# Four chunks of a fused attention and FFN kernel as two pairs: seven block products for eight, with weight sums streamed from HBM

## The chip, the cores and the metric

The kernel runs on one core of a Trainium2 chip. The core's engines run side by side, each with its own queue taken in order: TensorE (PE; PEld is its weight load), VectorE (DVE), ScalarE (ACT), GpSimd (POOL) and SyncE (SP), whose queue issues the DMAs. The metric is the device time of one execution in microseconds (us).

## The reference

```python
def attention(q, k, v, mem_k, mem_v):           # B 4, H 8, S 768, D 64
    for c in range(S // 32):                     # each 32 queries see 16 keys left, 8 right, 8 memory keys
        k_full = concat(mem_k, k[c*32-16 : c*32+32+8]); v_full = ...
        a = softmax(0.125 * q[c*32:c*32+32] @ k_full.T)
        out[c*32:c*32+32] = a @ v_full
x = out as (3072 tokens, 512)
h = x @ w_in                                     # 512 -> 2048, the first FFN matrix
g = s * relu(h)**2 + b
y = g @ w_out                                    # 2048 -> 512, the second
```

All in float32; a product is made of three TensorE matmuls on rounded high and low parts (low x high, high x low, high x high).

## The kernel before

The 3,072 tokens are 8 chunks of 384. A chunk needs 4 visits of attention (two heads each) and 16 steps of the FFN, one per slice f of 128 hidden units. A visit (`attend`, `weights`, `flip`) puts scores on TensorE (L383), maxima on VectorE (L440), exponentials on ScalarE (L444), a normalisation on GpSimd (L450), transposes on VectorE (L470) and values on TensorE (L415). From chunk 2 on, the values of one visit and the scores of the next are issued as one group.

A step is 12 matmuls of the hidden product (`hidden`, L510: 4 row blocks of the weight slice x 3 parts, 384 columns each), then relu, square, affine and the high part gH on ScalarE (L517 to L520), the low part gL on VectorE (L521), and 9 matmuls of the result (`result`, L532: 3 token tiles x 3 parts, 512 columns), one step later on TensorE. After the last step of a chunk the three accumulators are copied (L548) and stored.

The weights come as 64-bit floats. `weight` loads one 0.5 MB tile (L485) into one of 16 early tiles or a ring of four named words, joins the bits on ScalarE and VectorE (L487 to L492, through a ring wv) and leaves a high and a low part w (L496, L497). All 32 weight tiles then stay on chip.

`Plan` sets the order: every operation has a priority (in steps) and dependencies, and a list scheduler with a table of durations lays each engine's queue out before the program runs. On the chip each queue is then taken in that order. The planner keeps some VectorE and GpSimd operations (marked lock) apart.

Of the kernel before, what the change touches and what calls it, by code (L numbers as in the profile page):

```python
# [25 lines left out]
P = 128  # L26
# [38 lines left out]
SLOW, NSLOW = 290.0, 6
# [8 lines left out]
class Val:  # L74
# [170 lines left out]
@with_exitstack  # L245
def body(ctx: ExitStack, tc: tile.TileContext, qkv, w1, w2, out):
    nc = tc.nc
    plan = Plan()
    op = plan.op

# [10 lines left out]
    wts = {}  # L261
    early_tiles = [const.tile([P, 2 * DM], F32, name=f"early{i}", tag=f"slot{i}") for i in range(NEARLY)]

    def weight_tile(half, f):
        if (half, f) not in wts:
            i = LATE_W.index((half, f)) if (half, f) in LATE_W else -1
            wts[half, f] = const.tile([P, 2, DM], F32R, name=f"w{half}_{f}", tag=f"slot{i}" if i >= 0 else f"w{half}_{f}")
# [6 lines left out]
    xr = [[const.tile([P, TOK], F32R, name=f"x{a}{c}_{i}") for a in "HL" for c in range(NC_T)] for i in range(2)]  # L274
    x_ring = Ring(xr)
    wvs = ring("wv", 3, [P, DM], F32)
# [68 lines left out]
    def anchor(ch, c):  # L345

        if ch == 0:
            return -30 + 2 * c
        if ch < NALONE:
            return starts[ch] - LEAD - 2.0 * (H // 2 - 1 - c)  # L350
        return starts[ch] - JOIN - (4.0 if ch > NALONE else APART) * (H // 2 - c)

    x_vals, open_ = {}, []

    def attend(ch, c):
# [11 lines left out]
        due = a if alone else anchor(ch, c + 1)  # L367
# [18 lines left out]
        if alone:  # L386
            for j in range(GB):
                op("PE", "scores", a, lambda j=j: product(j), (raw[0],), (scs[0][j], scs[1][j]))
        else:

            last = open_.pop() if open_ else None
# [13 lines left out]
            (turn if early else flip)(a + n * 0.5, t[n], aT[n], ch == 1 or n == 1)  # L405

        va = Val(ps, "v")
        if c == 0:
            x_vals[ch] = Val(x_ring)
        x = x_vals[ch]  # L410
        av = lambda: va.tile[:, :TOK]

        def value(j):
# [2 lines left out]
                                 v.tile[:, (n * GB + j) * D:(n * GB + j + 1) * D], aT[n].tile[:, j, :], start=True, stop=True)  # L416

        def store():
            op("ACT", "xhigh", due + 0.9, lambda: nc.scalar.activation(x.tile[c], av(), AF.Copy), (va[0],), (x["H", c],))
            op("DVE", "xlow", due + 0.9, lambda: nc.vector.tensor_tensor(x.tile[NC_T + c], av(), x.tile[c].bitcast(F32), ALU.subtract),  # L420
               (va[0], x["H", c]), (x["L", c],))

        def values():
# [76 lines left out]

    g_vals, h_vals, a_vals, partial = {}, {}, {}, {}

    def hidden(u):
        ch, f = STEPS[u]
        h = Val(ps, "h")
        x, w = x_vals[ch], c_w[0, f]

        def products(c):
            for n, (wi, xi) in enumerate(((0, NC_T + c), (1, c), (0, c))):
                nc.tensor.matmul(h.tile[:, :TOK], weight_tile(0, f)[:, wi, c * P:(c + 1) * P], x.tile[xi], start=(c == 0 and n == 0),  # L510
                                 stop=(c == NC_T - 1 and n == 2))
# [5 lines left out]
        op("ACT", "relu", u, lambda: nc.scalar.activation(hp(), hp(), AF.Relu), (), (h[0],))  # L517
        op("ACT", "square", u, lambda: nc.scalar.activation(hp(), hp(), AF.Square), (), (h[0],))  # L518
        op("ACT", "affine", u, lambda: nc.scalar.activation(hp(), hp(), AF.Identity, scale=s_sb, bias=b_sb), (c_s[0], c_b[0]), (h[0],))  # L519
        op("ACT", "high", u, lambda: nc.scalar.activation(g.tile[0], hp(), AF.Copy), (h[0],), (g["H"],))  # L520
        op("DVE", "low", u, lambda: nc.vector.tensor_tensor(g.tile[1], hp(), g.tile[0].bitcast(F32), ALU.subtract),  # L521
           (h[0], g["H"]), (g["L"],))

    def result(u):
# [89 lines left out]
```

## Time and profile before

| | |
|---|---|
| median of 3 runs | 641.81 us (641.69 to 641.99) |
| span of the profiled execution, first to last instruction | 639.8 us |
| median of the runs less that span | 2.0 us |
| busy TensorE / VectorE / ScalarE / GpSimd | 625.7 / 354.8 / 422.4 / 86.9 us |
| DMA | 46.83 MB, mean 73 GB/s |

The busy times are sums over the profiled execution. Matmuls overlap, and their ends are modelled, so a busy TensorE can still have slack; what one matmul really costs is read from the distance of starts.

### The profile page before, as it was taken

Reading aid. Unit: us, or ns where it says so; the run is one execution under the profiler, and the core shown is the slowest. Engines: PE = TensorE matmul, PEld = TensorE weight load, DVE = VectorE, ACT = ScalarE, POOL = GpSimd, SP = SyncE. Lnnn points to the kernel's source line nnn. Section 1 sums busy time; section 2 is a strip of 40 time slices with the busy share of each in tenths; the row PEclk is TensorE's granted clock in tenths of the full one; section 3 lists DMA queues with packets and bytes.
Section 4 is the critical chain, followed back from the end, with each engine's and each line's share of the span. In section 5 each row is a group of like instructions: output and inputs, shape, how many; then the busy total and the mean of one; then the engine's idle time right before and its main releaser. Section 6 shows DMA issues by size and latency. Waiting matters only on the chain.

```text
span 639.8 us, 10842 instructions
## 1 busy us (share of the span) xinstructions
PE 625.7 (98%) x3822; PEld 544.2 (85%) x3826; DVE 354.8 (55%) x1283; ACT 422.4 (66%) x1137; POOL 86.9 (14%) x140
## 2 busy tenths in 40 slices
PE   9998988999999999999999999999999999999997
PEld 5686877888888898888888988889888888989995
DVE  5999999726667355563447554473555725421112
ACT  6999898756766566666566666664666665645543
POOL 4522100101211011110011111110111100100000
PEclk9999999999999999999999999999999999999999
DMA  8933664012112011121103011120111200010001
GB/s 336 404 112 114 212 207 152 2 46 83 58 46 96 5 41 47 47 95 47 45 2 105 37 46 46 46 96 1 45 47 47 96 17 1 1 50 1 1 0 50
DMA packets 17334, 46.83 MB, mean 73 GB/s; under 512 B 1920, under 2 KB 1920, under 8 KB 17280
## 3 DMA queue, kind: packets, MB, share of 16 engines
q1 hardware_dynamic: 17280, 46.15, 20.8%
q8 instruction: 30, 0.49, 0.3%
q14 instruction: 24, 0.20, 0.1%
HBM read 39.85 MB, written 6.29 MB: 72 GB/s over the span
## 4 chain that ended last, share of the span: by engine, by line
PE 80%; DVE 10%; ACT 6%; DMA 4%; issue 1%; SPq 0%; POOL 0%; DVEq 0%
PE ps L532 37%; PE ps L510 36%; PE ps L383 4%; PE ps L415 3%; DVE wv L490 2%; DVE w L497 2%; DVE wv L492 2%; DMA early<-w 2%; ACT t L444 1%; DMA v<-qkv 1%; DVE gL L521 1%; DVE words L488 1%; ACT wv L487 1%; DMA early<-qkv 1%; ACT ps L519 1%; ACT w L496 1%
## 5 line engine op out<-in xcount | busy, mean ns | idle before, releaser
L510 PE MATMUL ps<-xH,w 128*128 128x384 f32 x1024 | 261.8, 337 | 1.3 <-DVE w L497 1.3
L532 PE MATMUL ps<-w,gH 128*128 128x512 f32 x768 | 240.0, 393 | 0.6 <-DVE w L497 0.5
L510 PEld LDWEIGHTS ps<-xH,w 128*128 128x128 f32 x1024 | 186.0, 188 | 7.6 <-DVE w L497 2.4
L521 DVE TENSOR_TENSOR gL<-ps,gH 128x384 fp32r<-128x384 f32 x128 | 70.6, 552 | 208.8 <-ACT gH L520 207.6
L517 ACT ACTIVATE ps<-ps 128x384 f32<-128x384 f32 x128 | 60.9, 475 | 173.1 <-PE ps L510 173.1
L510 PE MATMUL ps<-xL,w 128*128 128x384 f32 x512 | 174.4, 341 | 0.0
L532 PEld LDWEIGHTS ps<-w,gH 128*128 128x128 f32 x768 | 144.0, 188 | 29.4 <-DVE w L497 1.3
L532 PE MATMUL ps<-w,gL 128*128 128x512 f32 x384 | 154.9, 403 | 6.6 <-DVE gL L521 6.6
L470 DVE STREAM_TRANSPOSE aT<-t 32x128 f32<-32x128 f32 x384 | 116.2, 303 | 51.1 <-POOL t L450 46.4
L444 ACT ACTIVATE t<-t,nmax 96x128 f32<-96x128 f32 x256 | 99.3, 390 | 17.2 <-DVE nmax L440 16.9
L510 PEld LDWEIGHTS ps<-xL,w 128*128 128x128 f32 x512 | 96.1, 188 | 6.6 <-ACT w L496 0.4
L532 PEld LDWEIGHTS ps<-w,gL 128*128 128x128 f32 x384 | 72.0, 188 | 24.5 <-DVE gL L521 9.6
L519 ACT ACTIVATE ps<-ps,b_sb,s_sb 128x384 f32<-128x384 f32 x128 | 82.6, 645 | 4.2
L450 POOL TENSOR_TENSOR t<-t,rden 96x512 f32<-96x512 f32 x64 | 68.5, 1070 | 85.8 <-DVE rden L449 85.8
L447 POOL TENSOR_SCALAR rden<-den 96x4 f32<-96x4 f32 x64 | 16.0, 251 | 375.5 <-ACT t L444 372.8
L520 ACT ACTIVATE gH<-ps 128x384 fp32r<-128x384 f32 x128 | 62.9, 491 | 3.9
L518 ACT ACTIVATE ps<-ps 128x384 f32<-128x384 f32 x128 | 60.8, 475 | 4.0
L440 DVE CUSTOM_DVE_ANT_0 t<-ps,mask 96x128 f32<-96x128 f32 x256 | 56.8, 281 | 4.2 <-PE ps L383 3.8
L444 ACT ACTIVATION_READ_ACCUMULATOR t<-t,nmax 96x1 f32 x256 | 48.1, 188 | 0.0
L383 PE MATMUL ps<-raw 64*96 64x128 f32 x448 | 31.8, 279 | 0.0
L383 PEld LDWEIGHTS ps<-raw 64*96 64x96 f32 x448 | 25.3, 159 | 4.1 <-issue 0.8
L415 PEld LDWEIGHTS ps<-aT,v 128*64 128x64 f32 x448 | 19.6, 136 | 7.9 <-issue 6.6
(45 smaller groups left out, 289.3 us busy)
## 6 DMA issues: line engine op xcount, KB each, us to landing
raw<-qkv SPq DMA_DIRECT2D x28, 448.0 KB, 3.3
words<-w SPq DMA_DIRECT2D x22, 512.0 KB, 3.9
v<-qkv SPq DMA_DIRECT2D x28, 256.0 KB, 3.6
out<-partial SPq DMA_DIRECT2D x21, 256.0 KB, 2.1
early<-w SPq DMA_DIRECT2D x10, 512.0 KB, 9.9
early<-qkv SPq DMA_DIRECT2D x3, 448.0 KB, 5.8
early<-qkv SPq DMA_DIRECT2D x4, 256.0 KB, 6.4
out<-wv SPq DMA_DIRECT2D x3, 256.0 KB, 3.8
```

The lines of the kernel that those rows point to most:

```text
L383: nc.tensor.matmul(scv(n)[:, j, :], raw.tile[rows, j * QB:(j + 1) * QB], raw.tile[rows, TOK + j * P:TOK + (j + 1) * P], start=True, stop=True)
L440: op("DVE", "max", a + 0.1, lambda j=j: nc.vector.tensor_tensor_reduce(t.tile[:, j, :], scv()[:, j, :], mask[:, kind(j)], -SCALE, 3.0e38, ...
L444: op("ACT", "exp", a + 0.2, lambda j=j: nc.scalar.activation(t.tile[:, j, :], t.tile[:, j, :], AF.Exp, bias=nmax()[:, j:j + 1], scale=-1.0 ...
L450: op("POOL", "norm", a + 0.25, lambda: nc.gpsimd.tensor_tensor(t.tile, t.tile, rden().unsqueeze(2).to_broadcast([QB, GB, P]), ALU.mult), [ ...
L470: nc.vector.transpose(aT.tile[gg, :, cs], t.tile[cs, :, gg])
L510: nc.tensor.matmul(h.tile[:, :TOK], weight_tile(0, f)[:, wi, c * P:(c + 1) * P], x.tile[xi], start=(c == 0 and n == 0), stop=(c == NC_T - ...
L517: op("ACT", "relu", u, lambda: nc.scalar.activation(hp(), hp(), AF.Relu), (), (h[0],))
L518: op("ACT", "square", u, lambda: nc.scalar.activation(hp(), hp(), AF.Square), (), (h[0],))
L519: op("ACT", "affine", u, lambda: nc.scalar.activation(hp(), hp(), AF.Identity, scale=s_sb, bias=b_sb), (c_s[0], c_b[0]), (h[0],))
L520: op("ACT", "high", u, lambda: nc.scalar.activation(g.tile[0], hp(), AF.Copy), (h[0],), (g["H"],))
L521: op("DVE", "low", u, lambda: nc.vector.tensor_tensor(g.tile[1], hp(), g.tile[0].bitcast(F32), ALU.subtract), (h[0], g["H"]), (g["L"],))
L532: nc.tensor.matmul(acc.tile, g.tile[gi][:, t * P:(t + 1) * P], weight_tile(1, f)[:, wi, :], start=(first and n == 0), stop=(last and n == 2))
```

## The change

Chunks 0 to 3 stay as they were. Chunks 4 and 5, and 6 and 7, become pairs. For a pair the first FFN matrix is computed two slices (f = 2g, 2g + 1) and two chunks at a time: the weights are a 2 x 2 block matrix A, the inputs a 2 x 2 block matrix B (rows: halves of the 512 inputs, columns: the two chunks), and the product is formed from seven block products in place of eight (`seven`). A block product is 6 matmuls of 384 columns.

- `blocks`: for each of 8 groups GpSimd rebuilds the full weights (2 additions of 512 columns, vsum), forms four sums S1 to S4 (4 of 256, ssum), ScalarE and VectorE cut them into high and low parts (1,024 columns each), and 11 DMAs store the group's seven blocks to HBM tiles w1s. 16 further DMAs store the second FFN matrix to w2s. The second matrix and the plain blocks A11, A12, A22 can be stored as soon as a weight tile is ready; the sums wait for all weights.
- `mix`: before a pair, four subtractions of 768 columns on GpSimd and seven cuts on ScalarE and VectorE make T1 to T4 and the parts of B11, B21 and B22, in the places of weight tiles that are no longer needed.
- `word`: weights come back from HBM, 28 tiles of 0.5 MB for the products and 32 for the results of each pair, into 8 slots in the places of old weight tiles.
- `seven`: per group 7 products, five additions on VectorE, a copy and relu on ScalarE, squares of 768 columns on GpSimd and a wide affine on ScalarE. P2 is added onto P1's bank and P4 onto P7's.
- `rest`: the result matmuls of the pair, 2 x 16 units of 9 matmuls, after all products, with gH and gL cut from the stored g.
- The order of the rest: visits of chunks 2 to 5 get anchors 2.3 steps apart from step 18 on, those of chunks 6 and 7 lie in the first pair; two visits are open in place of one (DEPTH); epilogues have a priority 8 steps earlier from step 22 on (AHEAD); wv has 5 buffers in place of 3.

```diff
+STEPS = (... [(ch, f) for ch in range(2, NPLAIN) for f in range(NF)])      # NPLAIN = 4, was NCHUNK
+BLOCKS = ("A11", "S2", "S1", "S3", "A12", "S4", "A22")
...
-        return starts[ch] - JOIN - (4.0 if ch > NALONE else APART) * (H // 2 - c)
+        i = (ch - NALONE) * (H // 2) + c
+        last = (NCHUNK - 2 - NALONE) * (H // 2)
+        if ch < NCHUNK - 2:
+            return VISITS[0] + VISITS[1] * i
+        return base(NCHUNK - 4) + LAST_VISITS[0] + LAST_VISITS[1] * (i - last)
...
+    def blocks(g):
+        full, sums, high, low = (Val(words) for _ in range(4))
...
+            op("POOL", "vsum", due, lambda k=k, f=f: nc.gpsimd.tensor_tensor(
+                at(full, 2 * k, 2), weight_tile(0, f)[:, 0].bitcast(F32), weight_tile(0, f)[:, 1].bitcast(F32), ALU.add),
+               [*parts[k], *all_w], (full[k],), lock=True)
...
+        op("ACT", "shigh", due, lambda: nc.scalar.activation(high.tile.bitcast(F32R), sums.tile, AF.Copy), every, (high[0],))
+        op("DVE", "slow", due, lambda: nc.vector.tensor_tensor(low.tile.bitcast(F32R), sums.tile, high.tile, ALU.subtract),
+           (*every, high[0]), (low[0],), lock=True)
...
+            put = lambda src, dst, reads, key: op("SP", "issue", due + 0.5, lambda: nc.sync.dma_start(dst, src()), reads,
+                                                  (c_w1s[unit][q, key],), size=P * 2 * P * 4)
...
+    def word(ch, n, prio):
+        v = Val(streams)
+        src, c_src = (w1s[n], c_w1s[n]) if n < NWORDS else (w2s[(n - NWORDS) % NF], c_w2s[(n - NWORDS) % NF])
...
+        op("SP", "issue", prio - 3.0, lambda: nc.sync.dma_start(v.tile.bitcast(F32), flat), list(c_src.parts.values()), [v[0], *gone], size=P * DM * 8)
...
+    def seven(ch, g):
...
+            more = name in ("P2", "P4")
+            bank = banks_[name] = banks_[{"P2": "P1", "P4": "P7"}[name]] if more else Val(ps, "p")
+            def matmuls():
+                for kc in range(2):
+                    for i, (wi, xi) in enumerate(((0, 1), (1, 0), (0, 0))):
+                        lo = q * DM + wi * 2 * P + kc * P
+                        nc.tensor.matmul(bank.tile[:, :TOK], w.tile[:, lo:lo + P], xv.tile[xi][:, kc], ...)
...
+        b1 = product("P1", "A11", "B11", 0)
+        op("ACT", "keep", due - AHEAD, lambda: nc.scalar.activation(sb(sa), pt(b1), AF.Copy), (b1[0],), (sa[0],))
+        b6 = product("P6", "S2", "T2", 1)
+        op("DVE", "add", due - AHEAD, lambda: nc.vector.tensor_tensor(sb(su), pt(b6), sb(sa), ALU.add), (b6[0], sa[0]), (su[0],))
+        b5 = product("P5", "S1", "T1", 2)
...
+            op("POOL", "square2", due + 2, lambda v=v: nc.gpsimd.tensor_tensor(v.tile, v.tile, v.tile, ALU.mult), (), (v[0], v[1]), lock=True)
...
+    def rest(ch, i):
+        w, src = word(ch, NWORDS + i, due), gv[c, f // 2]
...
+        op("ACT", "high", due - AHEAD, lambda: nc.scalar.activation(g.tile[0], part(), AF.Copy), (src[f % 2],), (g["H"],))
+        op("DVE", "low", due - AHEAD, lambda: nc.vector.tensor_tensor(g.tile[1], part(), g.tile[0].bitcast(F32), ALU.subtract),
+           (src[f % 2], g["H"]), (g["L"],), lock=True)
...
+    for f in range(NF):
+        op("SP", "issue", LATER + 1.5 * f, lambda f=f: nc.sync.dma_start(w2s[f], weight_tile(1, f).bitcast(F32)),
+           (c_w[1, f]["H"], c_w[1, f]["L"]), (c_w2s[f][0],), size=P * DM * 8)
...
+    for ch in range(NPLAIN, NCHUNK, 2):
+        visits(ch)
+        visits(ch + 1)
+        mix(ch)
+        for g in range(NF // 2):
+            seven(ch, g)
+        for i in range(2 * NF):
+            rest(ch, i)
```

Three places of the engines' queues show what moves. SyncE's queue while the weights are prepared, before: loads of weight tiles stand one behind the other.

```order
L485 DMA words_102<-w 128x1024
L485 DMA words_103<-w 128x1024
L485 DMA words_100<-w 128x1024
L485 DMA words_101<-w 128x1024
L369 DMA raw_105<-qkv 128x896
```

The same place now (w1s and w2s are the HBM tiles, w_5_828 and the like finished weight tiles):

```order
L633 DMA w1s_67<-w_5_828 128x2x256
L533 DMA words_140<-w 128x1024
L418 DMA v_150<-qkv 128x512
L830 DMA w2s_89<-w_4_865 128x1024
L533 DMA words_141<-w 128x1024
L533 DMA words_142<-w 128x1024
L633 DMA w1s_67<-w_6_902 128x2x256
L633 DMA w1s_69<-w_6_902 128x2x256
L830 DMA w2s_90<-w_5_909 128x1024
L533 DMA words_143<-w 128x1024
L633 DMA w1s_70<-w_7_963 128x2x256
```

Stores of finished tiles stand between the loads; between the fifth and the last words load there are 12 of w1s (0.26 MB) and 9 of w2s (0.52 MB).

VectorE's queue just after the last weight tile, before: maxima, transposes and gL alone.

```order
L449 RECIPROCAL rden_121<-rden_121 96x4
L521 TENSOR_TENSOR gL_133<-ps_143,gH_132 128x384
L470 STREAM_TRANSPOSE aT_113<-t_107 32x4x32 x8
L521 TENSOR_TENSOR gL_129<-ps_142,gH_128 128x384
L521 TENSOR_TENSOR gL_131<-ps_139,gH_130 128x384
```

There now (words are reused for the sums: 143 the sums, 140 their high part, 141 their low part):

```order
L497 RECIPROCAL rden_161<-rden_161 96x4
L572 TENSOR_TENSOR gL_173<-ps_183,gH_172 128x384
L518 STREAM_TRANSPOSE aT_153<-t_147 32x4x32 x8
L629 TENSOR_TENSOR words_141<-words_143,words_140 128x1024
L572 TENSOR_TENSOR gL_169<-ps_182,gH_168 128x384
L572 TENSOR_TENSOR gL_171<-ps_179,gH_170 128x384
L629 TENSOR_TENSOR words_141<-words_143,words_140 128x1024
```

The cuts of the weight sums (1,024 columns) stand between the gL, and the next visit's maxima follow two gL sooner.

TensorE's queue at the start of the second pair (before there was no such place: each chunk's hidden and result matmuls alternate). Names again_n are tiles in the places of old weights: again_0 is B11, again_1 B21, again_4 T2, and again_9 to again_11 are stream slots.

```order
L790 MATMUL ps_181<-again_9_3598,gL_173 128x512
L790 MATMUL ps_181<-again_9_3598,gH_172 128x512 x2
L740 MATMUL ps_183<-again_0_3188,again_10_3603 128x384
L740 MATMUL ps_183<-again_0_3187,again_10_3603 128x384 x2
L740 MATMUL ps_183<-again_1_3250,again_11_3642 128x384
L740 MATMUL ps_183<-again_1_3249,again_11_3642 128x384 x2
L740 MATMUL ps_182<-again_4_3607,again_10_3603 128x384
L740 MATMUL ps_182<-again_4_3606,again_10_3603 128x384 x2
```

Behind the last result matmuls of the first pair come P1, then P2 on the same bank, then P6; the last value group of chunk 7 stands 27 result matmuls ahead of P1. (Each product's rows appear twice in the queue, once for each half of the rows; one half is shown.)

## Rows read from the trace of the kernel before

**Rows 1.** The page: busy time by engine, and TensorE's granted clock in 40 slices.

```profile
PE 625.7 (98%) x3822; PEld 544.2 (85%) x3826; DVE 354.8 (55%) x1283; ACT 422.4 (66%) x1137; POOL 86.9 (14%) x140
...
PEclk9999999999999999999999999999999999999999
```

**Rows 2.** Chain of waits, 372 to 400 us: start, duration, what.

```profile
371.85 1.05 PE ps L383 x16
...
375.17 2.10 PE ps L510 x12
...
381.44 2.10 PE ps L532 x9
...
389.82 0.81 PE ps L415 x16
```

**Rows 3.** Windows: length, busy PE, PEld, DVE, ACT, POOL, clock, DMA share, GB/s.

```profile
9.00:27.00 18.00, 17.68 (x188) 12.08 (x189) 15.19 (x95) 17.64 (x77) 11.60 (x18) 1.00 1.03 408
57.00:105.00 48.00, 43.25 (x242) 35.92 (x243) 45.72 (x91) 43.58 (x94) 3.18 (x4) 1.00 0.61 207
113.00:205.00 92.00, 91.20 (x564) 80.42 (x565) 55.17 (x222) 61.29 (x177) 14.05 (x23) 1.00 0.17 58
205.00:560.00 355.00, 355.00 (x2175) 315.96 (x2174) 184.96 (x734) 222.75 (x612) 46.29 (x73) 1.00 0.13 43
```

**Rows 4.** Groups of instructions by line: count, busy us, mean ns, idle before.

```profile
L510 PE MATMUL ps<-xH,w 128*128 128x384 f32 x1024 | 261.8, 337 | 1.3 <-DVE w L497 1.3
...
L510 PE MATMUL ps<-xL,w 128*128 128x384 f32 x512 | 174.4, 341 | 0.0
...
L497 DVE TENSOR_TENSOR w<-wv,w 128x512 fp32r<-128x512 f32 x32 | 22.2, 693 | 1.7 <-ACT w L496 1.7
```

**Rows 5.** Timeline, 601 to 634 us: start, duration, engine, line, operation.

```profile
601.45 0.39 PE L532 MATMUL ps<-w,gL 128*128 128x512 f32 x1
...
601.65 0.47 ACT L517 ACTIVATE ps<-ps 128x384 f32<-128x384 f32 x1 [1.98 <-PE ps L510]
...
603.87 0.56 DVE L521 TENSOR_TENSOR gL<-ps,gH 128x384 fp32r<-128x384 f32 x1 [3.60 <-ACT gH L520]
...
605.64 0.40 PE L532 MATMUL ps<-w,gL 128*128 128x512 f32 x1
...
633.78 0.50 PE L532 MATMUL ps<-w,gL 128*128 128x512 f32 x1 [0.76 <-DVE gL L521]
```

**Rows 6.** Waits of TensorE, 113 to 200 us: total us, times, longest.

```profile
PE ps L532 <- DVE gL L521: 1.7, 2, 0.9
```

**Rows 7.** Timeline, 36 to 39 us: GpSimd's normalisation and VectorE's cut of a weight.

```profile
36.73 1.04 POOL L450 TENSOR_TENSOR t<-t,rden 96x512 f32<-96x512 f32 x1 [1.15 <-DVE rden L449]
...
37.35 0.97 DVE L497 TENSOR_TENSOR w<-wv,w 128x512 fp32r<-128x512 f32 x1
```

**Rows 8.** Timeline, 84 to 92 us: a weight load's issue and its first use.

```profile
84.34 1.67 SPq L485 DMA_DIRECT2D words<-w  x2
...
89.52 0.67 ACT L487 ACTIVATE wv<-words 128x512 f32<-128x512 f32 x1
```

**Rows 9.** DMA: issues in 73 to 105 us (landing us); queue in 560 to 640 us.

```profile
words<-w SPq DMA_DIRECT2D x13, 512.0 KB, 3.2
...
q1 hardware_dynamic: 864, 1.57, 5.3%
```

**Rows 10.** Timeline of a visit, 372 to 388 us, VectorE and ScalarE.

```profile
373.77 0.28 DVE L440 CUSTOM_DVE_ANT_0 t<-ps,mask 96x128 f32<-96x128 f32 x1
...
373.98 0.28 DVE L440 CUSTOM_DVE_ANT_0 t<-ps,mask 96x128 f32<-96x128 f32 x1
...
381.43 2.51 DVE L470 STREAM_TRANSPOSE aT<-t 32x128 f32<-32x128 f32 x8 [0.71 <-POOL t L450]
...
374.55 0.39 ACT L444 ACTIVATE t<-t,nmax 96x128 f32<-96x128 f32 x1
```

**Rows 11.** Waits of TensorE, 56 to 113 us.

```profile
PE ps L532 <- DVE gL L521: 5.1, 7, 0.9
```

More of the change, by code (lines that the diff above doesn't have):

```diff
@@ L389, in attend @@
         else:
[L391 removed]
+            last = open_.pop(0) if len(open_) >= DEPTH else None
             def both():
@@ new lines, in again, with again_x, later, old @@
+    def again(half, f, shape, dtype):
+        return lambda: const.tile(shape, dtype, name=f"again{half}_{f}", tag=weight_tag(half, f))
+    def again_x(old, c):
+        return lambda: const.tile([P, 2, TOK], F32, name=f"againx{old}_{c}", tag=f"x{c}_{x_vals[old].slot}")
+    def later(slots, shape, dtype):
+        return Ring(Lazy([again(*s, shape, dtype) if s[0] in (0, 1) else again_x(*s) for s in slots])), slots
+    def old(slot):
+        if slot[0] in (0, 1):
+            return list(c_w[slot].parts.values())
+        return [x_vals[slot[0]][a, slot[1]] for a in "HL"]
@@ new lines, in body, with first, mix, subtract @@
+    n_of = {}
+    def first(kind, slots):
+        n = n_of[kind] = n_of.get(kind, -1) + 1
+        return old(slots[n]) if n < len(slots) else []
+    XNAMES = ("B11", "B21", "B22", "T1", "T2", "T3", "T4")
+    xc = {}
+    def mix(ch):
+        due = base(ch) - 6.0
+        raw = {name: x_vals[ch + int(name[2]) - 1, int(name[1]) - 1] for name in ("B11", "B12", "B21", "B22")}
+        flat = lambda v: v.tile[:, :2 * TOK] if v.ring is words else v.tile.rearrange("p c t -> p (c t)")
+        both = lambda v: [v[0], v[1]] if v.ring is words else [v[0]]
+        def subtract(dst, a, b, writes, prio):
+            op("POOL", "tsum", due + prio, lambda: nc.gpsimd.tensor_tensor(flat(dst), flat(a), flat(b), ALU.subtract), [*both(a), *both(b)],
+               writes, lock=True)
+        def cut(name, v, prio):
+            n = XNAMES.index(name)
+            x = xc[name] = Val(xcs[n])
+            gone = [p for s in seven_slots[n] for p in old(s)] if ch == NPLAIN else []
+            whole = lambda k: x.tile[k].rearrange("p c t -> p (c t)")
+            op("ACT", "thigh", due + prio, lambda: nc.scalar.activation(whole(0), flat(v), AF.Copy), both(v), [x["H"], *gone])
+            op("DVE", "tlow", due + prio, lambda: nc.vector.tensor_tensor(whole(1), flat(v), whole(0).bitcast(F32), ALU.subtract),
+               [*both(v), x["H"]], [x["L"], *gone], lock=True)
+        def temp():
+            v = Val(temps)
+            return v, [v[0], *first("temp", temp_slots)]
+        cut("B11", raw["B11"], 0.0)
+        cut("B21", raw["B21"], 0.0)
+        cut("B22", raw["B22"], 0.0)
+        t1, w = temp()
+        subtract(t1, raw["B12"], raw["B11"], w, 0.1)
+        cut("T1", t1, 0.2)
+        subtract(raw["B12"], raw["B22"], raw["B12"], both(raw["B12"]), 0.2)
+        cut("T3", raw["B12"], 0.3)
+        t2, w = temp()
+        subtract(t2, raw["B22"], t1, w, 0.4)
+        cut("T2", t2, 0.5)
+        t4, w = temp()
+        subtract(t4, raw["B21"], t2, w, 0.6)
+        cut("T4", t4, 0.7)
@@ new lines, in rest, with products @@
+    def rest(ch, i):
+        c, f = ch + i // NF, i % NF
+        due = base(ch) + NF // 2 * GROUP + UNIT * i
+        w, src = word(ch, NWORDS + i, due), gv[c, f // 2]
+        g = Val(gs)
+        part = lambda: src.tile[:, f % 2]
+        op("ACT", "high", due - AHEAD, lambda: nc.scalar.activation(g.tile[0], part(), AF.Copy), (src[f % 2],), (g["H"],))
+        op("DVE", "low", due - AHEAD, lambda: nc.vector.tensor_tensor(g.tile[1], part(), g.tile[0].bitcast(F32), ALU.subtract),
+           (src[f % 2], g["H"]), (g["L"],), lock=True)
+        def products(acc, t):
+            for n, (gi, wi) in enumerate(((1, 0), (0, 1), (0, 0))):
+                nc.tensor.matmul(acc.tile, g.tile[gi][:, t * P:(t + 1) * P], w.tile[:, wi * DM:(wi + 1) * DM],
+                                 start=(f == 0 and n == 0), stop=(f == NF - 1 and n == 2))
+        for t in range(NT):
+            if f == 0:
+                a_vals[t] = Val(ps, "acc")
+            acc = a_vals[t]
+            op("PE", "result", due, lambda acc=acc, t=t: products(acc, t), (g["H"], g["L"], w[0]), (acc[0],))
+            if f < NF - 1:
+                continue
+            o = Val(outs)
+            op("DVE", "out", due, lambda acc=acc, o=o: nc.vector.tensor_copy(o.tile, acc.tile), (acc[0],), (o[0],))
+            row = c * TOK + t * P
+            op("SP", "issue", due, lambda o=o, row=row: nc.sync.dma_start(out[row:row + P, :], o.tile), (o[0],), (), size=P * DM * 4)
```

171 lines of the change are left out of this document (143 added, 28 removed).

## The prediction

> **What bounds the kernel now.** I read the page first: TensorE is busy for 98% of the span at a granted clock of 1.0 (2.4 GHz) in every slice [rows 1]. Busy TensorE time is no proof, so next the chain of waits over 28 us in the middle: nothing but TensorE, 12 hidden matmuls in 2.10 us, 9 result matmuls in 2.10 us, a visit in 0.81 + 1.05 us, end to end [rows 2]. So a matmul of 384 columns costs 0.175 us, one of 512 columns 0.233 us, and one step (one 128-wide slice of the FFN for one chunk) 4.2 us. The windows show where that holds: from 205 to 560 us TensorE never idles; from 113 to 205 us it idles 0.8 us; in 57 to 105 us it does, and there VectorE is busy for 45.7 of 48 us [rows 3]. That is the weight preparation (four VectorE operations per 0.5 MB weight tile, the last of them 0.69 us [rows 4]), and the DMA engines move only 207 GB/s in it, against 408 GB/s in a saturated stretch [rows 3]. The groups give the count: 1,024 + 512 hidden matmuls [rows 4], 192 per chunk.
>
> The span is 639.8 us and the median of the runs 641.8, so 2.0 us lie around the span; I make the sum on 641.8.
>
> **The change, part by part.**
>
> *Removed from TensorE.* Four chunks had 4 x 192 = 768 hidden matmuls. Two pairs now have 8 groups x 7 products x 6 matmuls = 336 each, 672 together, all of 384 columns with one weight load each as before. 96 x 0.175 = **-16.8 us**. The 9 result matmuls per slice and the visits stay. From 205 us on nothing else bounds the kernel [rows 3], so this comes off the end if TensorE stays fed.
>
> *The end.* Before, the last step waits 0.76 us for its own gL: squaring, scaling and cutting follow the last hidden product [rows 5]. In the new result stage these inputs were made three units ahead. **-0.8 us**. The copies and stores behind it stay.
>
> *Epilogues ahead of exponentials from step 22.* From 113 to 200 us TensorE waited twice for gL, at most 0.9 us each [rows 6]; the windows give 0.8 us of idle [rows 3]. **-0.4 us** (0 to -0.8).
>
> *Start of the second pair.* The order puts the last value group of chunk 7 only 27 result matmuls (3 x 2.10 = 6.3 us) ahead of P1, then P2, then P6. P2 adds onto P1's bank, so it waits until ScalarE has copied P1 away: an activation of 384 columns is 0.47 us, and a hop between engines about 0.2 us each way (TensorE goes on to the next product at 601.45 us, ScalarE starts on the last at 601.65 us [rows 5]): **+0.9 us**. P6 needs T2 = B22 - T1. From the last value: hop and copy 0.7, then on GpSimd B22 - B12 and T2, each 768 elements. The nearest row is its normalisation, 1.04 us for 512 [rows 7], so 1.6 us each (3.2 with a hop), then cut on ScalarE and VectorE, some 0.9 + 1.1 us by proportion, and three hops: about 6.7 us. P6 starts at 6.3 + 1.05 + 0.9 + 1.05 = 9.3 us. It fits with 2.6 us to spare, but the two cuts before it and the three copies of results stand ahead on VectorE; bounds 0 to +3.
>
> *Weight preparation, 57 to 105 us.* SyncE's queue now holds between its 18 weight loads 12 stores of 0.26 MB and 9 of 0.52 MB, 7.9 MB, that wait in order for finished weight tiles. The old traffic is 207 GB/s x 48 us = 9.9 MB. At 407 GB/s all 17.8 MB need 43.7 us of the 48: it fits, at 91%. A load issued at 84.34 us was first used at 89.52 us, and the median landing there is 3.2 us [rows 8, 9]: 2.0 us of slack; a store of 0.52 MB ahead of it costs 1.3 us. Three of the 18 loads have 1.05 MB of stores directly ahead (2.6 us), so 3 x 0.6 = 1.8 us is the price in the queue. **+1.0 us** (0 to +8, see the rival). That stores run near the rate of loads is borne out by the only ones there are: 1.57 MB took 5.3% of 16 engines' 80 us, 370 GB/s while busy [rows 9], against 408 / 1.03 = 396 GB/s for loads [rows 3]. No store with 1 KB pieces exists before.
>
> The Trainium skill (DMA: Bandwidth & Descriptors, Specifications) gives a limit of about 358 GB/s of HBM for one core; the 408 GB/s held for 18 us [rows 3] contradict it, and the measurement decides. By the page 17.8 MB would take an estimated 49.7 us, 1.7 us more than the window, and my sum would be 0.7 us higher.
>
> *Steps 20 to 54: denser visits and weight sums.* Visits for chunks 2 to 5 now come every 2.1 steps, that is every 2.1 x 4.2 + 1.9 = 10.8 us. VectorE per visit: 8 maxima at 0.21 pace, 16 transposes in 2 x 2.51, and a cut like gL's 0.56: 7.3 us [rows 5, 10]; plus 2.1 gL, 1.2, plus for one block the cut of 1,024 elements, 1.4 us from 0.69 for 512 [rows 4]: 9.9 of 10.8 us. ScalarE: 8 exponentials of 0.39 and a copy, 3.6 [rows 10]; plus 2.1 epilogues of some 2.1 us (from 601.65 us to gL's start at 603.87 us [rows 5]), plus 1.2 for the high parts: 9.2 us. GpSimd, 2.5 before, gets about 4.2 more. All fit, VectorE barely (60% in 113 to 205 us before [rows 3]). TensorE is in order, so it stalls where a transpose or a gL is late. A visit's transposes end 11 us after its scores [rows 2, 10]; with two visits open instead of one they may take 21 us, so ten are free. A gL has 1.2 us to spare (ready at 604.43 us, wanted at 605.64 us [rows 5]). Eight blocks put a 1.4 us operation in front of some gL, and it may itself wait for GpSimd: once a VectorE cut took 0.97 us instead of 0.69 while GpSimd's normalisation was running [rows 7]. Bound: 8 x 1.4 = 11 us, if each blocks a gL wholly; nothing if each falls in a gap. A visit's eight transposes are 0.315 us each, so a gL gets in between them in time; only the 1.4 us cuts are longer than the slack, and only by 0.2 us when they run alone. I take a value near the lower end: **+1.5 us** (0 to +11).
>
> The Trainium skill (SBUF — State Buffer, Who interferes with whom) says that a VectorE instruction with two SBUF inputs and a GpSimd instruction that reads SBUF exclude one another for their whole length. The 0.97 us of [rows 7] agree. This speaks against the change, which adds 86 such VectorE instructions (8 weight cuts, 14 x cuts, 64 result cuts) and some 90 GpSimd ones; by that rule alone, each of the 8 weight cuts waiting out a GpSimd addition of an estimated 1.04 us, some 8 us would come on top of my sum, and C below would be the forecast.
>
> *Hidden.* The streams: 60 tiles of 0.5 MB per pair, one per 2.1 us of TensorE, 250 GB/s of the 408 shown, with 8 slots, so issued 15 us before use; eight in flight at the full rate are 8 x 0.52 / 0.408 = 10 us. Without that cover each tile late costs its lateness. Per group of products (7.4 us of TensorE) GpSimd squares 2 x 1.6 us, ScalarE works some 4.5 us by proportion from 0.47 us for 384 columns [rows 5], VectorE adds 5 x 0.56 us; what they make is used at the earliest one group later. The mix for pair 1: chunk 5's last value stands six steps (25 us) ahead of P1.
>
> Sum: 641.8 - 16.8 - 0.8 - 0.4 + 0.9 + 1.0 + 1.5 = 627.2, say **627 us**.
>
> **The rivals.**
> *A, the forecast*: 621.5 to 629. Its lower end: no added stall and 2 us less of the 5.1 us for which TensorE waits for gL in 56 to 113 us [rows 11], since five wv buffers instead of three let ScalarE run ahead. Chance 0.62.
> *B, the weight window becomes bound by DMA*: if stores of 1 KB pieces move at 250 GB/s while loads keep 407, the window needs 24.4 + 31.4 = 55.8 us, +8; at 300, +2.6. For it: 91% load, one in-order queue. Against: the 370 GB/s. 629 to 635 us. Chance 0.12.
> *C, vector side too dense*: the 11 us of steps 20 to 54 in full, 637 us. For it: 9.9 of 10.8 us, and only 1.2 us of slack for a gL. Chance 0.15.
> *D, slower*: the mechanism of B further on. The window must grow by 17 us to eat the gain: 24.4 + 7.9 / r = 65 gives r = 194 GB/s. Below that the kernel is slower; at 150 GB/s 77 us, so about 655 us. Nothing in the rows is so slow. Chance 0.07.
> *E, the streams starve*: at 200 GB/s a tile takes 2.6 us against 2.1, 120 x 0.5 = 60 us. The rate that the rows show is twice that. Chance 0.02.
>
> **How the numbers follow.** A measurement of this kernel tells about 0.2% (1.3 us) from no change. A, B and C are faster by more: 0.89. D and E are slower: 0.09. The rest, 0.02, is a C or D that stops at the old time. The likeliest is A: 627 us. The range takes A, B and C with its bound: 621.5 to 637, some 0.85 of the chance.
>
> **What would show it.** Hidden matmuls 768 of 384 columns plus 672 in the products at the same 0.175 us; TensorE without idle slices past 120 us; the weight preparation ending near 116 us as before (later: B or D); 250 GB/s from about 290 us on; in steps 20 to 54 few waits of TensorE for gL or transposes (many of about 1 us: C); about 1 us at the second pair's start; the last result matmuls without a wait. I am wrong if loads of weights land later than 5 us in 57 to 105 us, if gL waits pass 5 us in total, or if result units wait for a stream.

## The result and the profile after

The changed kernel takes 632.06 us (median of 4 runs, 631.11 to 632.25), the kernel before 641.75 us beside it: ratio 0.9844, interval 0.9831 to 0.9858. That is 9.7 us faster; 14.6 were forecast. The profiled execution has a span of 629.3 us, 10.5 less than before, so it is compared with -14.6 too.

The page of the changed kernel (busy time by engine; then issues: count, KB, us to landing) answers to [rows 1]:

```profile
PE 611.6 (97%) x3730; PEld 526.0 (84%) x3730; DVE 424.2 (67%) x1369; ACT 406.1 (65%) x1063; POOL 200.1 (32%) x228
...
PEclk9999999999999999999999999999999999999999
...
L560 PE MATMUL ps<-x,w 128*128 128x384 f32 x768 | 148.5, 340 | 1.3 <-DVE w L545 1.1
...
L740 PE MATMUL ps<-again,again 128*128 128x384 f32 x672 | 118.8, 337 | 0.6 <-ACT wv L750 0.6
...
words<-w SPq DMA_DIRECT2D x22, 512.0 KB, 5.5
```

TensorE has 14.1 us less busy time and 17.7 us of idle time (629.3 - 611.6) instead of 14.1. The windows (length, busy PE, PEld, DVE, ACT, POOL, clock, DMA share, GB/s) say where; the first, second and third answer to [rows 3]:

```profile
57.00:105.00 48.00, 41.64 (x232) 34.20 (x233) 43.91 (x88) 41.51 (x91) 3.18 (x4) 1.00 0.97 348
113.00:205.00 92.00, 89.64 (x566) 78.66 (x566) 70.42 (x264) 68.62 (x197) 49.42 (x61) 1.00 0.42 139
205.00:354.00 149.00, 146.96 (x952) 128.76 (x951) 98.16 (x368) 102.15 (x287) 45.75 (x54) 1.00 0.30 100
370.00:450.00 80.00, 80.00 (x539) 72.66 (x539) 67.69 (x245) 55.68 (x148) 34.77 (x36) 1.00 0.79 267
460.00:540.00 80.00, 79.36 (x446) 70.62 (x445) 45.24 (x94) 38.21 (x71) 26.68 (x18) 1.00 0.76 259
```

Two stages got worse. In the weight preparation TensorE is busy 1.6 us less (41.64 for 43.25), VectorE too, and the DMA engines are at 97%. From 205 us to the first pair TensorE, which never idled there before, idles 2.0 us. The pairs themselves are nearly clean: TensorE is busy for 80.00 and 79.36 of 80 us, at 267 and 259 GB/s, and the second window holds the start of the second pair.

For all kernels I use one measure, window length less busy TensorE time. It is 6.5 us (57 to 120 us), 0.8 (120 to 350) and 0.0 (350 to 500) in the kernel before, and 8.3, 3.1 and 0.1 in the changed one. The expectations below speak of a "loss" instead: from start to next start of each matmul, what exceeds 0.175 us (384 columns) or 0.233 us (512), summed. It runs 3 to 4 us higher than the idle time. It also counts the change from one shape to another and the slower pace at a lower granted clock, which the idle time does not.

### The profile page after: what moved, and what is told of

It is laid out like the page before. It is cut to its first block, busy times and chain, and to the rows that moved or that the text cites. A ratio compares the mean times of both kernels' runs of the same rounds, so it can differ in the third digit from the quotient of the medians.

```text
span 629.3 us, 11231 instructions
## 1 busy us (share of the span) xinstructions
PE 611.6 (97%) x3730; PEld 526.0 (84%) x3730; DVE 424.2 (67%) x1369; ACT 406.1 (65%) x1063; POOL 200.1 (32%) x228
## 4 chain that ended last, share of the span: by engine, by line
PE 66%; DVE 14%; ACT 11%; DMA 3%; POOL 3%; issue 2%; ACTq 0%; DVEq 0%; POOLq 0%
PE ps L790 20%; PE ps L740 19%; PE ps L583 11%; PE ps L560 9%; ACT t L492 4%; DVE aT L518 4%; PE ps L425 3%; DMA words<-w 3%; PE ps L459 2%; DVE gL L572 2%; PE ps L341 2%; ACT ps L570 2%; DVE wv L538 1%; DVE wv L540 1%; DVE w L545 1%
## 5 line engine op out<-in xcount | busy, mean ns | idle before, releaser
L560 PE MATMUL ps<-x,w 128*128 128x384 f32 x768 | 148.5, 340 | 1.3 <-DVE w L545 1.1
L560 PEld LDWEIGHTS ps<-x,w 128*128 128x128 f32 x768 | 135.3, 188 | 9.1 <-DVE w L545 2.6
L583 PE MATMUL ps<-w,gH 128*128 128x512 f32 x384 | 120.3, 394 | 0.5 <-DVE w L545 0.5
L790 PE MATMUL ps<-again,gH 128*128 128x512 f32 x384 | 120.3, 394 | 0.0
L740 PE MATMUL ps<-again,again 128*128 128x384 f32 x672 | 118.8, 337 | 0.6 <-ACT wv L750 0.6
L740 PEld LDWEIGHTS ps<-again,again 128*128 128x128 f32 x672 | 116.5, 188 | 1.9 <-ACT wv L750 0.9
L583 PE MATMUL ps<-w,gL 128*128 128x512 f32 x192 | 78.4, 409 | 8.1 <-DVE gL L572 8.1
L583 PEld LDWEIGHTS ps<-w,gH 128*128 128x128 f32 x384 | 71.9, 188 | 15.6 <-DVE w L545 1.6
L790 PE MATMUL ps<-again,gL 128*128 128x512 f32 x192 | 76.3, 397 | 0.1
L568 ACT ACTIVATE ps<-ps 128x384 f32<-128x384 f32 x64 | 30.4, 474 | 25.9 <-PE ps L560 25.8
```

The costliest lines, as they stand in the source:

```text
L568: op("ACT", "relu", u - ahead, lambda: nc.scalar.activation(hp(), hp(), AF.Relu), (), (h[0],))
L583: nc.tensor.matmul(acc.tile, g.tile[gi][:, t * P:(t + 1) * P], weight_tile(1, f)[:, wi, :], start=(first and n == 0), stop=(last and n == 2))
L740: nc.tensor.matmul(bank.tile[:, :TOK], w.tile[:, lo:lo + P], xv.tile[xi][:, kc], start=(not more and kc == 0 and i == 0), stop=(kc == 1 an ...
L790: nc.tensor.matmul(acc.tile, g.tile[gi][:, t * P:(t + 1) * P], w.tile[:, wi * DM:(wi + 1) * DM], start=(f == 0 and n == 0), stop=(f == NF ...
```

## The experiments

Times are medians of 4 or 5 runs; idle is TensorE's in 57 to 120 and in 120 to 350 us of the profiled execution; clock is the mean granted clock of an execution, lowest to highest of the runs.

| kernel | us | ratio to before, interval | idle 57-120 | idle 120-350 | clock |
|---|---|---|---|---|---|
| changed kernel | 632.06 | 0.9844, 0.9831 to 0.9858 | 8.3 | 3.1 | 1.000 |
| e1_stores_late | 632.38 | 0.985, 0.9834 to 0.9867 | 7.0 | 4.8 | 0.996 to 1.000 |
| e5_stores_spread | 629.69 | 0.9808, 0.9795 to 0.9821 | 7.3 | 3.1 | 0.999 to 1.000 |
| e12_pool_queue | 638.74 | 0.9954, 0.9942 to 0.9967 | 9.9 | 4.6 | 0.994 to 0.997 |
| e2_no_sums | 631.88 | 0.9841, 0.9827 to 0.9856 | 8.7 | 2.9 | 1.000 |
| e3_costs | 632.70 | 0.9863, 0.9849 to 0.9878 | 9.5 | 2.4 | 0.999 to 1.000 |
| e6_exp_later | 631.78 | 0.9842, 0.9824 to 0.986 | 9.6 | 0.9 | 0.993 to 1.000 |
| e8_no_ahead | 634.02 | 0.9867, 0.9848 to 0.9885 | 8.8 | 3.0 | 0.995 to 1.000 |
| e7_both | 630.23 | 0.9815, 0.9802 to 0.9829 | 8.3 | 0.9 | 0.996 |
| e9_exp_later_from_18 | 630.91 | 0.9829, 0.9814 to 0.9844 | 8.9 | 1.7 | 0.995 to 0.997 |
| e11_exp_2us_later | 631.02 | 0.9823, 0.9804 to 0.9843 | 9.2 | 0.7 | 0.995 to 0.999 |
| e13_sums_held | 628.50 | 0.9798, 0.9785 to 0.9812 | 6.3 | 3.3 | 0.997 to 1.000 |
| e4_eight | 648.25 | 1.0099, 1.0084 to 1.0114 | 9.2 | 3.0 | 0.999 to 1.000 |

e4_eight has the same code as the changed kernel up to the pairs and idles 9.2 instead of 8.3 us in the first stage: some 0.9 us there is the difference of one execution from another. The clock matters as well: the two runs of e13 at 0.997 took 629.74 and 629.89 us, the three at 1.000 took 627.90 to 628.50.

**Are the products worth what they were counted at?** e4_eight

```diff
-                for kc in range(2):
+                for kc in (0, 1, 0, 1) if name == "P4" else (0, 1):
```

> The product P4 is accumulated twice in each group, 96 matmuls of 384 columns more, as many as eight products would need (outputs of chunks 4 to 7 are then not the reference's). If TensorE alone bounds the two pairs, the whole 96 x 0.175 = 16.8 us come back: 648.9 us, slower than the kernel before. Rival (part of the removed TensorE time had been replaced by waits for streams or vector work in the pairs): less than 14 us come back, below 646 us.

16.2 us came back (648.25 - 632.06), slower than before. The group of products holds 768 matmuls in 135.4 us against 672 in 118.8, 0.173 us for each of the 96. TensorE alone bounds the pairs.

**The weight preparation.** e1_stores_late, e5_stores_spread, e12_pool_queue

In e1 they are laid out behind the last weights, in e5 not before a time of the plan (`nb`, new), in e12 issued by GpSimd:

```diff
-           (c_w[1, f]["H"], c_w[1, f]["L"]), (c_w2s[f][0],), size=P * DM * 8)
+           (c_w[1, f]["H"], c_w[1, f]["L"], *all_w), (c_w2s[f][0],), size=P * DM * 8)
```

```diff
+           (c_w[1, f]["H"], c_w[1, f]["L"]), (c_w2s[f][0],), size=P * DM * 8, nb=220e3 + 7.5e3 * f)
```

```diff
-        op("SP", "issue", LATER + 1.5 * f, lambda f=f: nc.sync.dma_start(w2s[f], weight_tile(1, f).bitcast(F32)),
+        op("POOL", "issue", LATER + 1.5 * f, lambda f=f: nc.gpsimd.dma_start(w2s[f], weight_tile(1, f).bitcast(F32)),
```

The unsummed blocks of w1s go the same way, in e5 with `nb=150e3 + 20e3 * g`.

> All stores of w2s and of the unsummed w1s blocks wait for the last prepared weight tile; nothing else is changed. Theory S (the stores stand ahead of weight loads in one queue and on the same DMA engines, and this is the 2.4 us that TensorE loses more than before between 57 and 120 us): the weight loads land in about 3.2 us again, TensorE idles between 57 and 120 us about as in the kernel before, and the time falls by 2 to 2.5 us, to about 629.7 us. Rival W (the loss comes from the other order of vector work or the five buffers): no change, 632 us. If the moved 14 MB then collide with the loads of the visits or come too late for the pair, slower than 632 us.

> The stores of unsummed blocks and of w2s are planned no earlier than 150 us (then 20 us apart by group) and 220 us (then 7.5 us apart), where the DMA engines of the changed kernel move 75 to 150 GB/s, and not right behind the weight preparation as in e1_stores_late. Theory S (stores cost TensorE some 2 us between 57 and 120 us, and e1 lost the same again between 120 and 205 us because moved stores held up those of the sums, whose buffers the next sums need): the loss in 57 to 120 us is 9.8 to 10.5 us, that in 120 to 205 us about 2 us as in the changed kernel, and the time falls to about 630 us (629.3 to 630.8). Rival: the order that the plan lays out elsewhere shifts as well and eats it, 632 us.

> The changed kernel, with the stores of unsummed blocks and of w2s issued by GpSimd instead of SyncE; the bytes and about the times of the stores stay. If the loss in 57 to 120 us comes from stores that wait in SyncE's queue ahead of weight loads (order in one queue), the loss falls from 12.2 to 10.6 us or less and the time to about 630 us. Rival (it comes from sharing the DMA engines, which are busy for 97% there): the loss stays at 12 us or more and the time at 632 us or above.

DMA queue and issues (count, KB, us to landing) in 73 to 105 us, first the changed kernel (answering to [rows 9]), then e5_stores_spread:

```profile
q1 hardware_dynamic: 5002, 11.91, 99.9%
...
words<-w SPq DMA_DIRECT2D x12, 512.0 KB, 5.7
w2s<-w SPq DMA_DIRECT2D x6, 512.0 KB, 5.2
w1s<-w SPq DMA_DIRECT2D x9, 256.0 KB, 4.8
```

```profile
q1 hardware_dynamic: 1949, 6.82, 64.3%
...
words<-w SPq DMA_DIRECT2D x12, 512.0 KB, 3.8
```

And in e12_pool_queue:

```profile
words<-w SPq DMA_DIRECT2D x10, 512.0 KB, 5.0
```

With stores among them, the weight loads take 5.7 us to land, 3.8 without. What waits is ScalarE, the first to read a landed weight tile (waits of ScalarE, 57 to 120 us, changed kernel; the kernel before has no such DMA row, e5 one of 1.7 us and e1 one of 1.0):

```profile
ACT wv L535 <- DMA words<-w: 4.6, 8, 1.0
ACT w L544 <- DVE wv L540: 3.7, 4, 1.6
```

e1 won in that stage (7.0 us idle) and lost that right behind it (4.8 us idle for 3.1, and a granted clock of 0.93 in 160 to 180 us, behind a wait of TensorE of 2.4 us): SyncE's queue was then full of 14 MB of moved stores, the small stores of the sums stood among them, and their buffers came free late. VectorE, in order, stood still for one (waits of VectorE, 120 to 160 us, e1_stores_late):

```profile
DVE gL L572 <- ACT gH L571: 6.6, 5, 2.9
DVE words L629 <- DMA w1s<-words: 4.5, 1, 4.5
```

e5 puts them from 150 us on, where the DMA engines have room, and keeps the gain: 629.69 us, 2.4 us below the changed kernel, intervals apart. e12 was to tell the queue from the engines: SyncE's queue was freed of these stores, yet the loads still took 5.0 us in the same window. So 1.2 of the 1.9 us of delay stay without the order in one queue, which points to the sharing of the DMA engines; the queue may have the rest. The time of e12 tells neither, since e12 is 6.7 us slower than the changed kernel for a reason of its own: TensorE idles more in both stages, its granted clock is 0.95 from 57 to 120 us, and GpSimd waits in order for finished weight tiles with normalisations behind the store (waits of GpSimd, 57 to 125 us):

```profile
POOL w1s L633 <- DVE w L545: 29.7, 10, 4.9
```

**The dense visits.** e2_no_sums, e3_costs, e6_exp_later, e8_no_ahead

In e2 `blocks` lacks its operations vsum, ssum, shigh and slow, and unsummed pieces are stored in place of the sums. The edits of e3, e6 and e8:

```diff
-             small=240, prod=1062, add=480, wide=850, square2=1600, vsum=1230, ssum=620, shigh=930, slow=1143, tsum=1700, thigh=670, tlow=880, norm=1010, wrest=1290, issue=440)
+             small=240, prod=1062, add=480, wide=850, square2=1600, vsum=1300, ssum=740, shigh=1060, slow=1210, tsum=1850, thigh=840, tlow=930, norm=1040, wrest=1290, issue=440)
```

```diff
-                    d.ready = max(d.ready, free[e] if d.eng == e and not o.size else o.end)
+                    d.ready = max(d.ready, free[e] if d.eng == e and not o.size else o.end + (1000.0 if o.hold == HOLD["max"] else 0.0))
```

```diff
-NSLACK = 22
+NSLACK = 999
```

> The sums of weight blocks (six additions on GpSimd, one copy on ScalarE and one subtraction on VectorE per group, eight groups) are left out; unsummed blocks are stored and streamed in their place, so the outputs of chunks 4 to 7 are not the reference's, while stores, streams and TensorE's work stay. Theory P (these operations stand in front of epilogues, and cause the 1 us waits at 192, 228 and 275 us): the waits go and the time falls by 2.5 to 3.5 us, to about 629 us. Rival Q (the waits come from exponentials that the plan puts ahead of an epilogue on ScalarE, and from maxima that are late behind transposes on VectorE, which the denser visits bring by themselves): at least one or two of the waits stay, 631 to 632 us.

> Only the planner's durations for the new vector operations are set to what the trace shows (block additions 1.30 and 0.74 us in place of 1.23 and 0.62, their copy 1.06 for 0.93, their cut 1.21 for 1.14, the mix 1.85, 0.84 and 0.93 for 1.70, 0.67 and 0.88, the normalisation 1.04 for 1.01), so that another order is laid out. If the waits in steps 20 to 54 come from an order laid out for too short durations, two or three of the four waits of about 1 us go and the time is 629 to 630.5 us. Rival (the waits come from the density itself, whatever the order): 631.5 to 633 us.

> Only the plan's belief about maxima is changed: it takes them as done 1 us later, so that exponentials that would be ready about when an epilogue is are laid behind the epilogue on ScalarE. Theory Q (exponentials ahead of an epilogue wait for maxima that VectorE delivers late, and the epilogue with its gL comes 1 to 2 us late): the waits near 192, 228 and 275 us go, the loss in 120 to 300 us falls from 5.8 to 3 us or less, and the time is 629 to 630 us. Rival (VectorE itself is too full there, whatever stands ahead on ScalarE): the waits move elsewhere and the time stays at 631.5 to 633 us.

> The higher rank of epilogues from step 22 on is taken out for the plain chunks (the pairs keep theirs). If the rank is what keeps the denser visits from TensorE (theory Q), more epilogues stand behind exponentials and the loss in 120 to 354 us grows from 6.7 to 10 us or more: 635 us or slower. Rival, as the prediction's -0.4 us has it: within 1 us of 632 us.

Leaving out every sum and its cut changes nothing (631.88 us, 2.9 us idle in 120 to 350): in this order they are not what costs. e6, which changes an order alone, takes the idle time there from 3.1 to 0.9 us. The place at 275 us in the changed kernel shows why (timeline, TensorE, then VectorE and ScalarE):

```profile
269.81 1.56 PE L560 MATMUL ps<-x,w 128*128 128x384 f32 x8
...
276.50 0.50 PE L583 MATMUL ps<-w,gL 128*128 128x512 f32 x1 [0.93 <-DVE gL L572]
...
269.50 2.20 DVE L518 STREAM_TRANSPOSE aT<-t 32x128 f32<-32x128 f32 x7
271.73 0.29 DVE L488 CUSTOM_DVE_ANT_0 t<-ps,mask 96x128 f32<-96x128 f32 x1
...
275.89 0.56 DVE L572 TENSOR_TENSOR gL<-ps,gH 128x384 fp32r<-128x384 f32 x1 [1.53 <-ACT gH L571]
...
272.12 0.40 ACT L492 ACTIVATE t<-t,nmax 96x128 f32<-96x128 f32 x1 [3.73 <-DVE nmax L488]
...
273.68 0.47 ACT L568 ACTIVATE ps<-ps 128x384 f32<-128x384 f32 x1
```

The hidden product ends at 271.4 us; ScalarE has been idle since 268.4 (272.12 - 3.73). But its next instructions are four exponentials that wait for maxima, and these stand on VectorE behind transposes until 271.73. The epilogue starts at 273.68, 2.3 us late, and TensorE waits. The plan had believed the maxima would be there in time. The waits of TensorE at 193 us (1.07 us) and 229 us (0.85) have the same order: four exponentials stand ahead of the epilogue, which starts 2.2 us after its product. There the copy of a weight sum on ScalarE (1.06 us) and a weight cut on VectorE (1.19 us) come ahead of the exponentials and the maxima as well. This gain did not reach the time in e6 itself: its order also changed before 120 us, where it idles 9.6 us, and behind single waits of 1.8 and 2.4 us its granted clock is 0.83 from 90 to 100 and from 120 to 130 us. In the profiled execution TensorE idles 0.7 us less than in the changed kernel (17.0 for 17.7) and is busy 1.6 us longer (613.2 for 611.6); the expected 629 to 630 us missed. e3 shuffles both stages with no net gain.

Without the rank (the earlier priority of the epilogues; e8) TensorE's idle time behind 120 us is about the same (3.0 us for 3.1), but all of it is one wait (timeline, ScalarE, VectorE and TensorE; then windows as above):

```profile
195.53 0.49 ACT L571 ACTIVATE gH<-ps 128x384 fp32r<-128x384 f32 x1
...
192.49 2.69 DVE L629 TENSOR_TENSOR words<-words,words 128x1024 fp32r<-128x1024 f32 x1
...
195.10 2.51 DVE L518 STREAM_TRANSPOSE aT<-t 32x128 f32<-32x128 f32 x8
...
197.64 0.56 DVE L572 TENSOR_TENSOR gL<-ps,gH 128x384 fp32r<-128x384 f32 x1
...
198.25 0.80 PE L583 MATMUL ps<-w,gL 128*128 128x512 f32 x1 [3.03 <-DVE gL L572]
```

```profile
180.00:200.00 20.00, 16.97 (x126) 14.62 (x125) 17.27 (x63) 15.61 (x50) 16.29 (x18) 0.93 0.45 141
200.00:220.00 20.00, 20.00 (x114) 17.74 (x114) 15.11 (x57) 13.08 (x43) 11.29 (x15) 0.90 0.41 142
```

Here VectorE makes most of the wait: gH is ready at 196.02, but its gL stands behind the cut of a weight sum, 2.69 us beside GpSimd's additions (in the changed kernel seven of the eight cuts take 1.19 to 1.23 us, one 2.23), and behind eight transposes. The end time, 634.02 us, is mostly the clock's: TensorE is busy 2.7 us longer than in the changed kernel (614.3 for 611.6) and idles only 0.7 us more in the whole execution, and the one run of e8 at a mean clock of 1.000 took 631.41 us. So the rank is worth about 2 us here, less than I expected, and through the length of one wait rather than through the idle time.

**Together.** e7_both joins e5 and e6; e9_exp_later_from_18 does so only for visits due after step 18 (condition `o.prio > VISITS[0]`); e11_exp_2us_later has 2000.0 for 1000.0; e13_sums_held adds to e9

```diff
-               [*parts[k], *all_w], (full[k],), lock=True)
+               [*parts[k], *all_w], (full[k],), lock=True, nb=122000.0)
```

> The spread stores and the later exponentials together. If both theories hold and their places (57 to 120 us, and 120 to 300 us) do not touch, the gains add: 627 to 628.5 us. If only the stores count: 630 us. If neither: 632 us.

> The spread stores of e5_stores_spread, and the maxima taken as done 1 us later by the plan, but only for visits due after step 18, so that the order during the weight preparation stays that of e5_stores_spread. Theory Q: the loss in 57 to 120 us is 10.6 us as in e5_stores_spread, that in 120 to 354 us some 4.8 us as in e7_both instead of 6.8, and the time 627 to 628.5 us. Rival (what is won behind 120 us in e7_both is not independent of what it lost before): 629.5 to 630.5 us.

> As e9_exp_later_from_18, but with 2 us instead of 1. Theory Q with enough room at 1 us: the same as e9_exp_later_from_18 within 0.7 us. If exponentials laid too late now make transposes and values late: slower than that by 1 us or more. If 1 us was too little: faster by 0.5 to 1 us.

> As e9_exp_later_from_18, with the sums of weight blocks planned no earlier than 122 us, so that on GpSimd they stand behind the normalisations of the first visit of chunk 2. In e9_exp_later_from_18 three of them ran at 107 to 115 us beside the last weight preparation, where VectorE's instructions took 1.10 to 1.67 us in place of 0.42 to 0.69, TensorE waited 3.5 us for a gL, and its granted clock was 0.66 from 115 to 120 us. If that is the whole loss: 57 to 120 us back at 10 us, no fall of the clock, and 626 to 628 us, the fastest version. Rival (the sums only move the collision to the transposes of that visit): 629 to 631 us.

e7 and e9 did not add up: 630.23 and 630.91 us, no better than e5. Both win behind 120 us and lose before, in idle time and in clock. In e7 TensorE idles 1.3 us less than in e5 (15.7 for 17.0) but is busy 2.2 us longer (612.9 for 610.7): behind a wait of 2.42 us its granted clock is 0.87 from 115 to 120 and 0.89 from 120 to 130 us. In e9 sums of weight blocks run beside the last weight preparation, since on GpSimd nothing stands ahead of them (a place in the plan is an order, not a wait). GpSimd, VectorE and TensorE in e9_exp_later_from_18, and VectorE at the same place in e13_sums_held:

```profile
106.47 2.72 POOL L617 TENSOR_TENSOR words<-w 128x512 f32<-128x512 f32 x2 [39.00 <-DVE wv L541]
...
106.72 1.32 DVE L537 TENSOR_SCALAR words<-words 128x512 int32<-128x512 int32 x1
108.07 1.67 DVE L539 SCALAR_TENSOR_TENSOR wv<-wv,words 128x512 int32<-128x512 int32 x1
...
114.79 0.50 PE L584 MATMUL ps<-w,gL 128*128 128x512 f32 x1 [3.50 <-DVE gL L573]
```

```profile
107.62 0.42 DVE L537 TENSOR_SCALAR words<-words 128x512 int32<-128x512 int32 x1
108.07 0.69 DVE L539 SCALAR_TENSOR_TENSOR wv<-wv,words 128x512 int32<-128x512 int32 x1
```

With the sums held back the preparation idles 6.3 us, as before the change (6.5), and the granted clock stays at 1.00. e13 takes 628.50 us, the fastest of all, 3.6 below the changed kernel and 0.5 above the range expected; its interval overlaps that of e5. Between 120 and 350 us 3.3 us of idle time are back in other places, so the rival holds in part. The longest of these waits is made by a weight cut that takes 3.59 us beside GpSimd's sums (GpSimd, VectorE, TensorE in e13_sums_held; the gH of that gL was ready at 199.13):

```profile
196.93 2.59 POOL L617 TENSOR_TENSOR words<-w 128x512 f32<-128x512 f32 x2
...
197.01 3.59 DVE L630 TENSOR_TENSOR words<-words,words 128x1024 fp32r<-128x1024 f32 x1
...
202.43 0.56 DVE L573 TENSOR_TENSOR gL<-ps,gH 128x384 fp32r<-128x384 f32 x1
...
203.04 0.50 PE L584 MATMUL ps<-w,gL 128*128 128x512 f32 x1 [1.92 <-DVE gL L573]
```

So later exponentials removed idle time behind 120 us in e6, e7, e9 and e11, not in e13, and no run shows their 2 us in the end time. e11 shows that more than 1 us changes nothing in the time.

## Why the prediction was right, and where it was off

The direction, the range (621.5 to 637) and the place of the gain held. The time lies outside the band of case A, which had a chance of 0.62, and inside that of B, by a bit of B and a bit of C rather than by either in full.

- *Removed from TensorE, -16.8.* Held: the two groups of 768 and 672 matmuls, 16.2 us back in e4.
- *The end, -0.8.* Held. The chain of waits of the changed kernel ends without a wait: 288 result matmuls in one piece.

```profile
499.37 1.05 PE ps L740 x6
...
500.45 0.50 ACT wv L750
...
500.99 57.56 PE ps L740 x330
558.55 67.07 PE ps L790 x288
...
625.64 0.69 DVE partial L801
```

- *Start of the second pair, +0.9.* The mechanism held, the size was less: the same rows show P2 waiting for ScalarE's copy of P1, 0.58 us idle (500.99 - 499.37 - 1.05 = 0.57). P6 did not wait for T2.
- *Weight preparation, +1.0.* Mis-sized: TensorE's idle time grew from 6.5 to 8.3 us, +1.8; two kernels with the stores moved have 7.0 and 7.3, so 1.0 to 1.3 of it is the stores' in idle time, and the time of e5 says 2.4; the rest of the 1.8 is within the 0.9 us between executions. The step that failed is "it fits, at 91%": I gave the mix the 407 GB/s of loads alone. Mixed, the engines are 99.9% busy and move 372 GB/s (11.91 MB in 32 us); 17.8 MB then need 47.8 of the 48 us. I had priced the stores as a queue ("1.8 us is the price in the queue"); the 5.0 us of e12 point to shared engines for most of it. This is rival B at its mild end. Loads landing in 5.7 us passed my own mark of 5 us. So did the gL waits, 8.1 us in all, but that mark was badly set: before the change they are 6.6 us in all, 5.1 of them before 113 us [rows 11].
- *Steps 20 to 54, +1.5, and the rank, -0.4.* Together +1.1; measured +2.3 (0.8 to 3.1 us). The failed step is the cause: I counted VectorE's share and blamed the 1.4 us cuts ("only the 1.4 us cuts are longer than the slack"). They take 1.19 to 1.23 us when they run alone, and e2 shows that in this order they cost nothing. What I left out is ScalarE's order: exponentials ahead of an epilogue hand VectorE's lateness on to a gL. Rival C named the right symptom, with the wrong mechanism for this order; in the orders of e8 and e13 a lengthened cut does make the longest wait. I also had gL getting in between a visit's eight transposes, and in e8 it stands behind all eight.
- *Hidden: the streams.* Held: 259 to 267 GB/s against 250 worked out, and no result unit waited.

The sum: idle time +3.6 us where the terms gave +2.2, that is 1.4 of the 4.1 us missed in the profiled execution. The other 2.7 lie in busy time, -14.1 instead of -16.8. About 0.5 of it is in the first 57 us (55.12 for 54.64, with 433 matmul records for 430); each wait also hides a little under the last matmul's modelled end (at 276.50 us: 12 matmuls fill 2.26 us, not 2.10). e4 gave 16.2 instead of 16.8 back, which may be 0.6 of it. The rest stays open. The median lies another 0.9 us above the profiled execution.

The rule on exclusive use of SBUF (SBUF — State Buffer, Who interferes with whom, of the Trainium skill) agrees with e9's 1.67 us for 0.69 (L539, two inputs in SBUF) beside GpSimd's sums. The 3.59 us for 1.19 of a weight cut in e13 agree too. The 8 us that I had worked out for the case that each weight cut waits did not come: in the changed kernel one of the eight was lengthened, by 1.0 us, and all sums together cost nothing that e2 could measure.

## What to carry to other kernels

A transfer that is "hidden" has to be summed with everything else in its window at the rate of that mix, and put where the engines are idle: the same 14 MB cost 1 us or more beside the weight loads, as much right behind them, and nothing that the idle time shows when spread from 150 us on. When a stage gets denser, look at what each in-order engine has queued ahead of the instruction that the bottleneck waits for: a busy share says little, and four exponentials ahead of one epilogue cost a wait of 0.9 us here. Moving one order shifts others, so judge each edit by its stage as well as by the end time. Look at the length of single waits and at the granted clock too: e8 idles as long as the changed kernel behind 120 us, in one wait instead of four, and is 2 us slower.

## What was not expected of the hardware

After a long wait TensorE's granted clock fell. In e9_exp_later_from_18, after 3.5 us idle, it is 0.66 from 115 to 120 us, that is partly the lower level of 1.2 GHz, and 12 hidden matmuls fill 3.05 us there instead of 2.26; the changed kernel, whose longest wait past 57 us is 1.5 us, shows 1.00 throughout. e1, e6, e7, e8, e11 and e12 show a fall too, behind waits of 1.8 to 3.5 us; the waits of 1.92 us in e13 and 1.98 us in e3 were followed by 1.00.

```profile
111.00:115.00 4.00, 0.50 (x3) 0.21 (x2) 3.93 (x6) 2.37 (x5) 2.22 (x2) 1.00 0.00 2
115.00:120.00 5.00, 5.00 (x18) 4.39 (x18) 4.81 (x22) 2.37 (x7) 0.00 (x0) 0.66 0.02 5
...
117.76 3.05 PE L561 MATMUL ps<-x,w 128*128 128x384 f32 x12
```

The clock differs between executions of one kernel: three runs of e8 at a mean granted clock of 0.995 took 633.8 to 634.5 us, one at 1.000 took 631.41.
